# One transposed reciprocal row and one result tile per attention unit

## The chip, the cores and the metric

The kernel runs on one core of a Trainium2 chip. The metric is device time in microseconds (us) of one execution. The engines that matter are TensorE (PE; PEld is its weight load), VectorE (DVE), ScalarE (ACT), GpSimd (POOL) and SyncE (SP), which issues every DMA of this kernel, in program order.

## The reference

Three stages follow one another. The attention has 4 batches, 8 heads, 576 positions and head size 64; two gated layers of 2304 tokens by 512 come after it.

```python
scores = scale * np.matmul(q, k.transpose(0, 1, 3, 2)) + bias     # bias per head, from the distance of positions
scores = scores - np.max(scores, axis=-1, keepdims=True)
attn = np.exp(scores)
attn = attn / (np.sum(attn, axis=-1, keepdims=True) + 1e-09)
x = np.matmul(attn, v)                                            # to (2304, 512)
h = x @ w_in;  x = (h - np.tanh(h)) @ w_out                       # 512 -> 2048 -> 512
y = (1 / (1 + np.exp(-(x @ w_gate))) * (x @ w_val)) @ w_out2      # 512 -> 1536 -> 512
```

All is float32. Where products are split into a high and a low part, that is the kernel's way to keep the precision.

## The kernel before, in words

The attention works on 16 units; a unit is a pair of heads (`hp`, 0 to 3) of one batch (`b`, 0 to 3). The 2 x 576 query rows of a unit are cut into 9 tiles of 128 rows: tiles 0 to 7 are four blocks of 128 rows of the two heads in turn, tile 8 holds the last 64 rows of both. A unit takes five steps (`STEP_TILES`): two tiles in each of the first four, tile 8 in the fifth. The loop over `sg` counts steps; one pass issues work of several units in a fixed lag, so that while one unit's scores are multiplied (`scores`, L226), the step before gets its exponentials (`expo`, L247), the one three steps back is transposed (`transposes`, L278 and L284), the one four steps back is copied from PSUM (`settle`, L297, `settle5`, L302), and the product with v is run in small portions (`pv_steps`, L314 and L317). There is no scheduler: each engine runs its instructions in the order of this code and waits where data or a buffer is not ready.

`expo` also sums the exponentials of each row. `stats` (L252, L253) takes 1/(sum + 1e-9) three times a unit, for tiles 0 to 3, tiles 4 to 7 and tile 8. The value of a row then stands on the row's partition, while the product with v has the rows along its columns. So `stats` stores the values, 4 bytes each, to a scratch array `rec` in DRAM (L258 twice for each group of four tiles, L256 twice for tile 8), and `spread` loads them back as rows, one for each head, each to 64 partitions (L263, tile `rt`): 256 columns for tiles 0 to 3, 320 for the rest. `evac` copies the product from PSUM (L321), multiplies it by `rt` on POOL (L322) and stores it to `xs` (L324), for the 256 and the 320 columns apart.

The raw q and k of a unit are loaded (L171) two units ahead, into one buffer each: ACT casts them to the high part (`high`, L183) in the first and second step of the unit before, POOL subtracts for the low part (`low`, L187) two steps later, and the load of the next raw array follows that subtraction. v is loaded at L177. In the units with `b` = 3, number 3, 7 and 11, the bias tiles of the next pair of heads are loaded from DRAM too (L164, 13 DMAs). Each unit also loads and splits one block of weights for the later layers (L487). `PVN`, `KIND`, `PREP` and the lags in the loop set which piece goes into which step.

The layers that follow (L567 on) load `xs`, and run on PE nearly without a gap.

Of the kernel before, what the change touches and what calls it, by code (L numbers as in the profile page):

```python
# [7 lines left out]
F32 = mybir.dt.float32  # L8
# [3 lines left out]
AF = mybir.ActivationFunctionType  # L12
# [119 lines left out]
NU = NP * NB  # L132
STEP_TILES = ((0, 1), (2, 3), (4, 5), (6, 7), (8,))
NS = len(STEP_TILES)
PREP = {0: ("high", 0), 1: ("high", 1), 2: ("low", 0), 3: ("low", 1)}
GROUP = (0, 0, 1, 1, 2)
GW = (256, 320)
QK = S + 64

# [1 line left out]
def attention_phase(tc, qT, kT, vP, ident_d, par, c_log, bsc, recs, xs, after_bias, load_weight, filler, tail):  # L141
# [4 lines left out]
    V, A, G, T = nc.vector, nc.scalar, nc.gpsimd, nc.tensor  # L146
    with ExitStack() as st, ExitStack() as early:
        right = lambda n, k: st.enter_context(tc.tile_pool(name=n, bufs=k, side="right"))
        vp, np_, sm, xp, rp = right("p1v", 3), right("p1n", NBUF - 1), right("p1m", 4), right("p1x", 2), right("p1r", 2)
        left = lambda n, k: early.enter_context(tc.tile_pool(name=n, bufs=k))  # L150
        after_bias()
        bp, qp, stg = left("p1b", 1), left("p1q", 2), left("p1s", 1)
# [58 lines left out]
        for _ in range(ALONE):  # L211
            next(bias_steps)

        npair, n8, ntile, nmin, nsum, rt, sc, at, tr, tf = ({} for _ in range(10))

        def scores(u, s):
            (qh, ql), (kh, kl) = prep[u]
# [10 lines left out]
        def reduce_min(u, t):  # L228
            s = sc.pop((u, t))
            if t == 8:  # L230
                n = n8[u] = np_.tile([128, S], F32, name="n8", bufs=1)
            else:
                if t % 2 == 0:
                    npair[u, t // 2] = np_.tile([128, 2 * S], F32, name="n")
                n = npair[u, t // 2][:, S * (t % 2):S * (t % 2) + S]
            if t % 4 == 0:
                nmin[u, t // 4] = sm.tile([128, 4], F32, name="mn")
                nsum[u, t // 4] = sm.tile([128, 4], F32, name="sums")
            m = nmin[u, t // 4][:, t % 4:t % 4 + 1]
            V.tensor_tensor_reduce(n.rearrange("p (a b) -> p a b", a=2), s[:, :, 0:288],  # L240
                                   bias[t].rearrange("p (a b) -> p a b", a=2), -0.125, 3.0e38, ALU.add, ALU.min, m)
            ntile[u, t] = n

        def expo(u, t):
            n = ntile.pop((u, t))
            m = nmin[u, t // 4][:, t % 4:t % 4 + 1]
            A.activation(n, n, AF.Exp, bias=m, scale=-1.0, accum_out=nsum[u, t // 4][:, t % 4:t % 4 + 1])  # L247

        def stats(u, g):
            w = 1 if g == 2 else 4  # L250
            r = sm.tile([128, 4], F32, name="rec")
            V.tensor_scalar(r[:, 0:w], nsum[u, g][:, 0:w], 1e-9, None, ALU.add)  # L252
            V.reciprocal(r[:, 0:w], r[:, 0:w])  # L253
            for a in range(2):
                if g == 2:
                    nc.sync.dma_start(dram_ap(recs[u, 1], GW[1] * a + 256, [[1, 64], [1, 1]]), r[64 * a:64 * a + 64, 0:1])  # L256
                else:
                    nc.sync.dma_start(dram_ap(recs[u, g], GW[g] * a, [[1, 128], [128, 2]]), r[:, a:4:2])  # L258

        def spread(u, g):  # L260

            r = rt[u, g] = rp.tile([128, 320], F32, name="rt")
            nc.sync.dma_start(r[:, 0:GW[g]], dram_ap(recs[u, g], 0, [[GW[g], 2], [0, D], [1, GW[g]]]))  # L263

        def transposes(u, s):


            t = STEP_TILES[s][0]
            if t in (0, 4):
                w = 2 * GW[t // 4]  # L270
                at[u, t // 4] = [at_pool.tile([128, 4, w], F32, name=f"at{t}"), at_pool.tile([128, w // 2], F32, name=f"a5{t}")]
            half = (slice(0, 64), slice(64, 128))
            pt = [ps_t.tile([128, 4, 2, 64], F32, name="pt") for _ in range(2)]
            n = n8.pop(u) if s == 4 else npair.pop((u, s))
            for i in range(4):
                for x in (0,) if s == 4 else (0, S + 64):
                    for r in range(2):
                        T.transpose(pt[r][:, i, x // S], n[half[r], x + 128 * i:x + 128 * i + 128], ident[half[r], half[r]])  # L278
            if s == 4:
                for a in range(2):  # L280
                    T.matmul(tf[u, 8][half[a], 128:192], n[:, 512:S], ident[:, half[a]], start=True, stop=True)
            else:
                pf = tf[u, min(t + 1, 7) + (t + 1) // 7] = ps_f.tile([128, 192], F32, name="pf")
                T.transpose(pf[:, 0:128], n[:, 512:640], ident)  # L284
            tr[u, s] = pt

        def place5(w, t):
# [16 lines left out]
        def pv_steps(u, g):  # L304
            hp, b = units[u]
            v = vs.pop(u) if g else vs[u]
            main, rest = at[u, g]
            N = GW[g]
            p = []

            def mm(c):
                if c == 0:
                    p.append(ps_v.tile([128, 512], F32, name="pv"))
                    T.matmul(p[0][:, 0:N], v[:, 4].rearrange("p a d -> p (a d)"), rest, start=True, stop=False)  # L314
                    return
                for a in range(2):
                    T.matmul(p[0][64 * a:64 * a + 64, 0:N], v[:, c - 1, a], main[:, c - 1, a * N:a * N + N], start=False, stop=(c == 4))  # L317

            def evac():
                x = xp.tile([128, 320], F32, name="x")  # L320
                A.copy(x[:, 0:N], p[0][:, 0:N])  # L321
                G.tensor_tensor(x[:, 0:N], x[:, 0:N], rt.pop((u, g))[:, 0:N], ALU.mult)  # L322
                c0 = b * S + 256 * g
                nc.sync.dma_start(xs[128 * hp:128 * hp + 128, c0:c0 + N], x[:, 0:N])  # L324
            return [lambda c=c: mm(c) for c in range(5)] + [evac]

        pvq, late = [], []
        for sg in range(NU * NS + TAIL):
            u, s = divmod(sg, NS)
            if sg == 3:  # L330
                assert next(bias_steps, 1) == 1
                p0.close()
                at_pool = right("p1a", 1)
                ps_t, ps_f, ps_v = psr(st, "ps_t", 2), psr(st, "ps_f", 1), psr(st, "ps_v", 1)

            def at_lag(lag):
                z = sg - lag
                return divmod(z, NS) if 0 <= z < NU * NS else None
            for f in late:
                f()  # L340
            late = []
            z = at_lag(4)
            if z:
                for t in STEP_TILES[z[1]]:
                    settle5(z[0], t)
                settle(*z)
            if sg < NU * NS:
                filler(s, "V")
            y = at_lag(2)
            if y and y[1] in (1, 3, 4):  # L350
                stats(y[0], GROUP[y[1]])
            x = at_lag(3)
            if x and x[1] in (1, 4):
                spread(x[0], x[1] // 4)
            y = at_lag(1)
            if y:
                for t in STEP_TILES[y[1]]:
                    expo(y[0], t)
            if sg < NU * NS:
                scores(u, s)  # L360
                for _ in range(PER[sg] if sg < NS else 0):
                    next(bias_steps, None)
                hp, b = units[u]
                for t in STEP_TILES[s]:
                    reduce_min(u, t)
                    if b == NB - 1 and hp + 1 < NP:
                        load_bias(hp + 1, t)
            y = at_lag(3)
            if z and z[1] in (1, 4):
                pvq += pv_steps(z[0], z[1] // 4)  # L370
            steps = PVN[s] if sg < NU * NS + 3 else 5
            if y:
                transposes(*y)
            for _ in range(steps):
                if pvq:
                    pvq.pop(0)()
                    if pvq and pvq[0].__name__ == "evac":
                        late.append(pvq.pop(0))
                        break
            if s == 0 and u + 1 < NU:  # L380
                alloc(u + 1)
            if s == 3 and u + 1 < NU:
                load_v(u + 1)
            if s in PREP and 1 <= u + 1 < NU:
                k, i = PREP[s]
                if k == "high":
                    high(u + 1, i)
                else:
                    low(u + 1, i)
                    if u + 2 < NU:  # L390
                        load_raw(u + 2, i)
            if sg < NU * NS:
                filler(s, "AGv")
            if sg == NU * NS:
                early.close()
            tail(sg - NU * NS)
# [392 lines left out]
def tile_attention_then_two_mlps(ctx: ExitStack, tc: tile.TileContext, qT, kT, vP, par, wi, wo, wg, wv, wo2, c_log, ident, out, xs=None):  # L789
# [3 lines left out]
    if xs is None:  # L793
        xs = dp.tile([DM, NT], F32, name="xs")
    x2s = dp.tile([DM, NT], F32, name="x2s")
    recs = {(u, g): dp.tile([2, GW[g]], F32, name=f"rec{u}_{g}") for u in range(NU) for g in range(2)}
    with tc.manual_schedule():
        con = ctx.enter_context(tc.tile_pool(name="con", bufs=1))
        cst = []
# [100 lines left out]
```

## Time and profile before

| what | value |
|---|---|
| median of 3 runs (lowest, highest) | 1359.73 us (1355.46, 1360.43) |
| the profiled execution's own time | 1357.28 us |
| its span in the trace | 1355.1 us |
| PE busy | 1176.0 us, 87% |
| DVE, ACT, POOL busy | 682.6, 619.2, 428.3 us |
| DMA | 117.22 MB, 97394 packets, of them 28560 under 512 B |

Times in the trace are microseconds from the start of the span. A busy share is an average over stages with different limits, so the stretch from 72 to 502 us, in which the units of the attention run, is to be read apart from the rest. A wait is put down to the one that came last; "issue" in a chain or a wait means that nothing in the profile explains it. In the page's slices PE is full only in the second half:

```
PE   5676386577757589999999999999999999999998
PEclk9887688777877799999999999999999999999999
DMA  6677867766886632333334333243110101000000
```

Each digit is a fortieth of the span in tenths: the share in which PE was busy, the granted TensorE clock, and the share in which the DMA engines were busy.

### The profile page before, as it was taken

The numbers are of one execution on the slowest core, as the hardware profiler recorded it, in microseconds if no ns is written. First come the engines' busy times: TensorE is split into PE (matmuls) and PEld (weight loads), VectorE is DVE, ScalarE is ACT, GpSimd is POOL, SyncE is SP. The second block draws the span as 40 slices with busy tenths as digits, with TensorE's granted clock in tenths as the row PEclk, the third lists the DMA queues.
The fourth block names the chain that finished last, engine by engine and source line by source line (L and its number), as shares of the span: only waits on it lengthen the run. The fifth ranks groups of instructions, "written<-read, shape, count | busy, mean of one in ns | idle before, by whom it ended". The sixth has DMA issues, their size and how long they took to land.

```text
span 1355.1 us, 20411 instructions
## 1 busy us (share of the span) xinstructions
PE 1176.0 (87%) x7760; PEld 1023.8 (76%) x7760; DVE 682.6 (50%) x1222; ACT 619.2 (46%) x1241; POOL 428.3 (32%) x391
## 2 busy tenths in 40 slices
PE   5676386577757589999999999999999999999998
PEld 2254254344434369999999999999999999999997
DVE  8954255335534439888888886687410000000000
ACT  7955264354435447777776665643221121211111
POOL 1012122122212225555555553445412121212211
PEclk9887688777877799999999999999999999999999
DMA  6677867766886632333334333243110101000000
GB/s 223 235 109 83 127 87 102 109 114 89 97 120 89 72 64 70 111 111 114 116 111 142 125 127 110 73 132 113 45 41 7 36 13 35 12 19 29 1 24 24
DMA packets 97394, 117.22 MB, mean 86 GB/s; under 512 B 28560, under 2 KB 75920, under 8 KB 97296
## 3 DMA queue, kind: packets, MB, share of 16 engines
q1 hardware_dynamic: 97296, 115.92, 39.1%
q8 instruction: 61, 1.00, 0.3%
q14 instruction: 37, 0.30, 0.1%
HBM read 86.04 MB, written 29.84 MB: 86 GB/s over the span
## 4 chain that ended last, share of the span: by engine, by line
PE 64%; DMA 3%; DVE 1%; ACT 1%; issue 0%; SPq 0%; POOL 0%; DVEq 0%; ACTq 0%
PE up L584 36%; PE acc L663 14%; PE acc L671 11%; DMA xm<-xs 1%; PE pv L317 1%; DMA rec<-rec 1%; DMA raw<-in_qT 1%; PE sc L226 1%; PE pt L278 0%; ACT z L605 0%; DMA wraw<-in_wv 0%; DVE up L630 0%; DVE t L627 0%; DVE up L625 0%; DVE up L628 0%
## 5 line engine op out<-in xcount | busy, mean ns | idle before, releaser
L584 PE MATMUL up<-xt,w 128*128 128x384 f32 x2880 | 520.6, 335 | 0.6 <-DVE t L631 0.6
L584 PEld LDWEIGHTS up<-xt,w 128*128 128x128 f32 x2880 | 503.3, 188 | 8.5 <-issue 1.8
L641 POOL TENSOR_TENSOR gl<-t,gh 128x384 fp32r<-128x384 f32 x168 | 175.6, 1055 | 471.6 <-ACT gh L640 337.5
L663 PE MATMUL acc<-gh,w 128*128 128x384 f32 x768 | 195.7, 335 | 2.9 <-ACT z L605 2.9
L633 DVE TENSOR_TENSOR t<-up,t 128x384 f32<-128x384 f32 x72 | 40.0, 556 | 309.4 <-ACT t L612 309.4
L612 ACT ACTIVATE t<-up 128x384 f32<-128x384 f32 x72 | 35.4, 492 | 339.7 <-PE up L584 339.7
L278 PE MATMUL pt<-ident,n 64*128 64x64 f32 x1152 | 63.0, 248 | 123.3 <-ACT at L297 123.1
L240 DVE CUSTOM_DVE_ANT_0 n<-sc,bias 128x576 f32<-128x576 f32 x144 | 104.0, 754 | 127.0 <-PE sc L226 105.9
L278 PEld LDWEIGHTS pt<-ident,n 64*128 64x128 f32 x1152 | 54.0, 156 | 133.9 <-ACT at L297 127.9
L663 PEld LDWEIGHTS acc<-gh,w 128*128 128x128 f32 x768 | 138.1, 188 | 4.8 <-ACT z L605 3.8
L671 PE MATMUL acc<-w,gh 128*128 128x512 f32 x432 | 134.3, 392 | 0.0
L663 PE MATMUL acc<-gl,w 128*128 128x384 f32 x384 | 128.3, 334 | 0.0
L322 POOL TENSOR_TENSOR x<-x,rt 128x256 f32<-128x256 f32 (+1 forms) x32 | 25.6, 799 | 291.2 <-ACT x L321 216.4
L247 ACT ACTIVATE n<-n,mn 128x576 f32<-128x576 f32 x144 | 111.7, 784 | 3.9 <-DVE mn L240 3.9
L527 POOL TENSOR_TENSOR w<-wu,w 128x512 fp32r<-128x512 f32 x68 | 96.5, 1421 | 6.4 <-ACT w L529 6.4
L317 PE MATMUL pv<-at,vs 128*64 128x320 f32 (+1 forms) x512 | 95.3, 491 | 0.2 <-DVE at L294 0.2
L574 POOL TENSOR_TENSOR xt<-xm,xt 128x384 fp32r<-128x384 f32 x72 | 73.8, 1039 | 66.7 <-ACT xt L573 66.7
L671 PEld LDWEIGHTS acc<-w,gh 128*128 128x128 f32 x432 | 80.1, 188 | 13.5
L640 ACT CAST gh<-t 128x384 fp32r<-128x384 f32 x168 | 84.8, 511 | 8.5 <-PE acc L663 3.6
L297 DVE COPY at<-pt 128x512 f32<-128x512 f32 x64 | 44.0, 687 | 86.7 <-PE pt L278 81.3
L671 PE MATMUL acc<-w,gl 128*128 128x512 f32 x216 | 85.4, 395 | 0.0
L626 ACT ACTIVATE z<-z,c 128x768 f32<-128x768 f32 x48 | 45.2, 941 | 77.4 <-DVE up L625 77.4
(69 smaller groups left out, 1560.6 us busy)
## 6 DMA issues: line engine op xcount, KB each, us to landing
wraw<-in_wo SPq DMA_DIRECT2D x28, 512.0 KB
bsc<-e SPq DMA_DIRECT2D x36, 295.5 KB
xm<-xs SPq DMA_DIRECT2D x48, 192.0 KB
x2s<-o SPq DMA_DIRECT2D x48, 192.0 KB
wraw<-in_wi SPq DMA_DIRECT2D x16, 512.0 KB
wraw<-in_wg SPq DMA_DIRECT2D x12, 512.0 KB
wraw<-in_wv SPq DMA_DIRECT2D x12, 512.0 KB
raw<-in_qT SPq DMA_DIRECT2D x16, 320.0 KB
```

Of the source, the lines that this page charges most:

```text
L240: V.tensor_tensor_reduce(n.rearrange("p (a b) -> p a b", a=2), s[:, :, 0:288], bias[t].rearrange("p (a b) -> p a b", a=2), -0.125, 3.0e38, ...
L247: A.activation(n, n, AF.Exp, bias=m, scale=-1.0, accum_out=nsum[u, t // 4][:, t % 4:t % 4 + 1])
L278: T.transpose(pt[r][:, i, x // S], n[half[r], x + 128 * i:x + 128 * i + 128], ident[half[r], half[r]])
L317: T.matmul(p[0][64 * a:64 * a + 64, 0:N], v[:, c - 1, a], main[:, c - 1, a * N:a * N + N], start=False, stop=(c == 4))
L527: self.nc.gpsimd.tensor_sub(w[:, 1], u, w[:, 0].bitcast(F32))
L574: G.tensor_sub(t[:, 1], m, t[:, 0].bitcast(F32))
L584: T.matmul(p[:, 0:TB], w[:, a, 128 * kt:128 * kt + 128], x[:, c], start=(kt == 0 and i == 0), stop=(kt == 3 and i == 2))
L626: A.activation(z, z, AF.Relu, bias=nz, scale=-1.0)
L640: A.copy(h, x[:, j])
L641: G.tensor_sub(l, x[:, j], h.bitcast(F32))
L663: T.matmul(ac[blk][d][:, 0:TB], w[:, a, 128 * d:128 * d + 128], c, start=(begin and j == 0 and i == 0), stop=(end and j == NPR - 1 and i = ...
L671: T.matmul(ac[blk][d], g[:, c], w[:, a], start=(begin and i == 0), stop=(end and i == 2))
```

## The change

1/sum is now taken once a unit for all nine tiles, as 9 columns of one tile (`stats`); `COL` gives the column of each tile, so that a head's four tiles stand side by side. One TensorE transpose turns the 128 x 9 values into 9 rows of 128 in the PSUM tile that the unit's last full transpose uses anyway. `flat` copies these rows to SBUF on ACT and stores them in three DMAs: four rows of 512 bytes for each head, and the last row in two pieces of 256 bytes. `spread` loads them back in one DMA of 576 columns. The product with v is copied into one tile of 576 columns from two PSUM tiles; `close` multiplies it once and stores it once. `flat`, `spread` and `close` come 7, 8 and 11 steps after a unit's first, so in the third and fourth step of the next unit and the second of the one after it. The pools of the two tiles are opened later, once the bias phase has closed.

```diff
-            if t % 4 == 0:
-                nmin[u, t // 4] = sm.tile([128, 4], F32, name="mn")
-                nsum[u, t // 4] = sm.tile([128, 4], F32, name="sums")
+            if t == 0:
+                nmin[u], nsum[u] = (sm.tile([128, 9], F32, name=x) for x in ("mn", "sums"))
...
-        def stats(u, g):
-            w = 1 if g == 2 else 4
-            r = sm.tile([128, 4], F32, name="rec")
-            V.tensor_scalar(r[:, 0:w], nsum[u, g][:, 0:w], 1e-9, None, ALU.add)
-            V.reciprocal(r[:, 0:w], r[:, 0:w])
+        def stats(u):
+            r = nrec[u] = sm.tile([128, 9], F32, name="rec", bufs=2)
+            V.tensor_scalar(r, nsum.pop(u), 1e-9, None, ALU.add)
+            V.reciprocal(r, r)
+        def flat(u):
+            r = xp.tile([9, 128], F32, name="rr")
+            A.copy(r, tf[u, 8][0:9, 192:320])
             for a in range(2):
-                if g == 2:
-                    nc.sync.dma_start(dram_ap(recs[u, 1], GW[1] * a + 256, [[1, 64], [1, 1]]), r[64 * a:64 * a + 64, 0:1])
-                else:
-                    nc.sync.dma_start(dram_ap(recs[u, g], GW[g] * a, [[1, 128], [128, 2]]), r[:, a:4:2])
-        def spread(u, g):
-            r = rt[u, g] = rp.tile([128, 320], F32, name="rt")
-            nc.sync.dma_start(r[:, 0:GW[g]], dram_ap(recs[u, g], 0, [[GW[g], 2], [0, D], [1, GW[g]]]))
+                nc.sync.dma_start(dram_ap(recs[u], S * a, [[128, 4], [1, 128]]), r[4 * a:4 * a + 4])
+            nc.sync.dma_start(dram_ap(recs[u], 512, [[0, 1], [S, 2], [1, 64]]), r[8:9].rearrange("p (a q) -> p a q", a=2))
+        def spread(u):
+            r = rt[u] = rp.tile([128, S], F32, name="rt")
+            nc.sync.dma_start(r, dram_ap(recs[u], 0, [[S, 2], [0, D], [1, S]]))
+        def close(u):
+            hp, b = units[u]
+            x = xo.pop(u)
+            G.tensor_tensor(x, x, rt.pop(u), ALU.mult)
+            nc.sync.dma_start(xs[128 * hp:128 * hp + 128, b * S:b * S + S], x)
...
                 T.transpose(pf[:, 0:128], n[:, 512:640], ident)
+                if s == 3:
+                    T.transpose(pf[0:9, 192:320], nrec.pop(u), ident)
...
             def evac():
-                x = xp.tile([128, 320], F32, name="x")
-                A.copy(x[:, 0:N], p[0][:, 0:N])
-                G.tensor_tensor(x[:, 0:N], x[:, 0:N], rt.pop((u, g))[:, 0:N], ALU.mult)
-                c0 = b * S + 256 * g
-                nc.sync.dma_start(xs[128 * hp:128 * hp + 128, c0:c0 + N], x[:, 0:N])
+                if g == 0:
+                    xo[u] = xp.tile([128, S], F32, name="x")
+                A.copy(xo[u][:, 256 * g:256 * g + N], p[0][:, 0:N])
...
-            if y and y[1] in (1, 3, 4):
-                stats(y[0], GROUP[y[1]])
-            x = at_lag(3)
-            if x and x[1] in (1, 4):
-                spread(x[0], x[1] // 4)
+            if y and y[1] == 4:
+                stats(y[0])
+            for lag, f in ((7, flat), (8, spread), (11, close)):
+                x = sg - lag
+                if 0 <= x < NU * NS and x % NS == 0:
+                    f(x // NS)
```

The queue of SyncE around unit 8's reciprocals, before: `rec_0_80` and `rec_1_81` are the two scratch arrays of unit 8, `raw`, `vs` the loads of q, k and v for later units, `wraw` a weight block.

```order
L258 DMA rec_0_80<-rec 128x2x1 x2
L177 DMA vs<-in_vP 128x640
L171 DMA raw_3227<-in_kT 128x640
L263 DMA rt<-rec_0_80 128x1x256
L258 DMA rec_1_81<-rec 128x2x1 x2
L324 DMA xs<-x 128x320
L256 DMA rec_1_81<-rec 64x1 x2
L487 DMA wraw<-in_wo 128x1024
L263 DMA rt<-rec_1_81 128x1x320
L171 DMA raw_3439<-in_qT 128x640
L324 DMA xs<-x 128x256
```

The same place of the same queue in the changed kernel (`rec_72` is unit 8's scratch array, `rr` the nine rows; its lines have moved by a few numbers, L494 is L487 of before, L269 is L324).

```order
L269 DMA xs<-x 128x576
L494 DMA wraw<-in_wo 128x1024
L257 DMA rec_72<-rr 4x128 x2
L258 DMA rec_72<-rr 2x1x64
L171 DMA raw_3287<-in_qT 128x640
L263 DMA rt<-rec_72 128x1x576
L177 DMA vs<-in_vP 128x640
L171 DMA raw_3344<-in_kT 128x640
L269 DMA xs<-x 128x576
```

Six stores of `rec`, two loads of `rt` and two stores of `xs` have become three, one and one. The load of raw q, which stood behind a load of `rt`, now stands ahead of it; v and raw k stand right behind it. The first store of `rec` has moved from ahead of v to behind the weight block.

On ACT, around the cast of kh in a unit, before (`at` is the copy of transposed tiles, `n` and `sums` the exponentials, `x` the copy of the product):

```order
L183 CAST kh<-raw_2108 128x640
L297 COPY at_2186<-pt 128x8x64
L247 ACTIVATE n,sums<-n,mn 128x576 x2
L321 COPY x<-pv 128x256
```

The same place now:

```order
L183 CAST kh<-raw_2026 128x640
L305 COPY at_2095<-pt 128x8x64
L255 COPY rr<-pf 9x128
L245 ACTIVATE n,sums<-n,mn 128x576 x2
L330 COPY x<-pv 128x256
```

The copy of the nine rows has come in behind the cast of kh and one copy of `at`; the rest has kept its order.

## Rows read from the trace of the kernel before

**Rows 1.** Stretches: us, their length, busy us of engines (instructions), granted clock, DMA share, GB/s.

```profile
72.06:447.38 375.32, 248.67 (x2377) 166.10 (x2376) 173.58 (x465) 178.84 (x449) 89.85 (x83) 0.78 0.73 100
441.29:455.91 14.62, 14.62 (x173) 10.14 (x171) 11.82 (x35) 11.47 (x30) 5.02 (x5) 1.00 0.67 63
...
501.83:1355.10 853.27, 846.01 (x4644) 815.38 (x4644) 426.28 (x561) 358.60 (x627) 320.11 (x289) 1.00 0.21 70
```

**Rows 2.** Waits, 72.06 to 447.38: engine, line, for what, total us, times, longest.

```profile
ACT qh L183 <- DMA raw<-in_qT: 117.5, 13, 23.3
ACT kh L183 <- DMA raw<-in_kT: 45.1, 13, 8.5
...
PE pt L278 <- ACT at L297: 120.3, 23, 19.5
...
SPq L263 <- DMA rec<-rec: 179.6, 31, 8.8
```

**Rows 3.** Timeline of an ordinary unit: start, us, instruction, [idle before, releaser].

```profile
194.40 1.14 SPq L256 DMA_DIRECT2D rec<-rec  x2
...
204.55 0.55 SPq L263 DMA_DIRECT2D rt<-rec  x1
...
211.59 0.72 ACT L183 CAST qh<-raw 128x640 fp32r<-128x640 f32 x1 [6.71 <-DMA raw<-in_qT]
```

**Rows 4.** Timeline of SyncE, DVE and ACT at the first rec stores.

```profile
71.83 1.16 SPq L164 DMA_DIRECT2D bias<-bsc  x2
73.10 0.53 SPq L171 DMA_DIRECT2D raw<-in_qT  x1
73.73 0.89 SPq L258 DMA_DIRECT2D rec<-rec  x2
...
75.17 0.43 SPq L171 DMA_DIRECT2D raw<-in_kT  x1
83.23 0.61 SPq L263 DMA_DIRECT2D rt<-rec  x1
...
76.03 0.76 DVE L240 CUSTOM_DVE_ANT_0 n<-sc,bias 128x576 f32<-128x576 f32 x1 [4.93 <-DMA bias<-bsc]
...
77.60 0.71 ACT L183 CAST qh<-raw 128x640 fp32r<-128x640 f32 x1
...
86.19 0.72 ACT L183 CAST kh<-raw 128x640 fp32r<-128x640 f32 x1 [3.97 <-DMA raw<-in_kT]
```

**Rows 5.** Stretches of one us around them; the last two columns are DMA.

```profile
68.00:69.00 1.00, 1.00 (x25) 1.00 (x24) 0.16 (x2) 1.00 (x4) 0.00 (x0) 1.00 1.04 399
...
80.00:81.00 1.00, 1.00 (x4) 0.35 (x5) 1.00 (x3) 1.00 (x3) 0.00 (x0) 0.50 0.44 10
...
86.00:87.00 1.00, 0.00 (x0) 0.00 (x0) 0.13 (x2) 0.81 (x2) 0.00 (x0) 1.00 0.27 50
```

**Rows 6.** Groups by line and form, 72.06 to 447.38: busy us, mean ns, idle before.

```profile
L297 ACT COPY at<-pt 128x512 f32<-128x512 f32 x57 | 33.9, 595 | 0.0
...
L284 PE MATMUL pf<-ident,n 128*128 128x128 f32 x57 | 20.8, 364 | 0.0
L302 ACT COPY a<-pf 128x128 f32<-128x128 f32 x43 | 11.5, 268 | 3.2 <-PE pf L284 3.2
L322 POOL TENSOR_TENSOR x<-x,rt 128x320 f32<-128x320 f32 x13 | 11.2, 861 | 136.1 <-ACT x L321 136.1
L322 POOL TENSOR_TENSOR x<-x,rt 128x256 f32<-128x256 f32 x14 | 10.3, 735 | 129.8 <-ACT x L321 61.7 <-DMA rt<-rec 30.6 <-ACT n L247 17.1
```

**Rows 7.** Timeline: a load of rt and the multiplication that waits for it.

```profile
192.28 0.52 SPq L263 DMA_DIRECT2D rt<-rec  x1
...
202.49 0.73 POOL L322 TENSOR_TENSOR x<-x,rt 128x256 f32<-128x256 f32 x1 [10.64 <-DMA rt<-rec]
```

**Rows 8.** Unit 15: a stretch as in rows 1, and ACT's timeline.

```profile
455.91:475.77 19.86, 4.29 (x37) 2.32 (x35) 2.67 (x9) 3.54 (x9) 2.67 (x3) 0.60 0.64 80
...
470.99 0.51 ACT L573 CAST xt<-xm 128x384 fp32r<-128x384 f32 x1 [16.43 <-DMA xm<-xs]
```

More of the change, by code (lines that the diff above doesn't have):

```diff
@@ L135 @@
 PREP = {0: ("high", 0), 1: ("high", 1), 2: ("low", 0), 3: ("low", 1)}
-GROUP = (0, 0, 1, 1, 2)
+COL = [slice(c, c + 1) for c in (0, 4, 1, 5, 2, 6, 3, 7, 8)]
 GW = (256, 320)
@@ L148, in attention_phase @@
         right = lambda n, k: st.enter_context(tc.tile_pool(name=n, bufs=k, side="right"))
-        vp, np_, sm, xp, rp = right("p1v", 3), right("p1n", NBUF - 1), right("p1m", 4), right("p1x", 2), right("p1r", 2)
+        vp, np_, sm = right("p1v", 3), right("p1n", NBUF - 1), right("p1m", 4)
         left = lambda n, k: early.enter_context(tc.tile_pool(name=n, bufs=k))
@@ L212, in attention_phase @@
             next(bias_steps)
-        npair, n8, ntile, nmin, nsum, rt, sc, at, tr, tf = ({} for _ in range(10))
+        npair, n8, ntile, nmin, nsum, nrec, rt, xo, sc, at, tr, tf = ({} for _ in range(12))
         def scores(u, s):
@@ L235, in reduce_min @@
                 n = npair[u, t // 2][:, S * (t % 2):S * (t % 2) + S]
-            if t % 4 == 0:
-                nmin[u, t // 4] = sm.tile([128, 4], F32, name="mn")
-                nsum[u, t // 4] = sm.tile([128, 4], F32, name="sums")
-            m = nmin[u, t // 4][:, t % 4:t % 4 + 1]
+            if t == 0:
+                nmin[u], nsum[u] = (sm.tile([128, 9], F32, name=x) for x in ("mn", "sums"))
+            m = nmin[u][:, COL[t]]
             V.tensor_tensor_reduce(n.rearrange("p (a b) -> p a b", a=2), s[:, :, 0:288],
@@ L245, in expo @@
             n = ntile.pop((u, t))
-            m = nmin[u, t // 4][:, t % 4:t % 4 + 1]
-            A.activation(n, n, AF.Exp, bias=m, scale=-1.0, accum_out=nsum[u, t // 4][:, t % 4:t % 4 + 1])
-        def stats(u, g):
-            w = 1 if g == 2 else 4
-            r = sm.tile([128, 4], F32, name="rec")
-            V.tensor_scalar(r[:, 0:w], nsum[u, g][:, 0:w], 1e-9, None, ALU.add)
-            V.reciprocal(r[:, 0:w], r[:, 0:w])
-            for a in range(2):
-                if g == 2:
-                    nc.sync.dma_start(dram_ap(recs[u, 1], GW[1] * a + 256, [[1, 64], [1, 1]]), r[64 * a:64 * a + 64, 0:1])
-                else:
-                    nc.sync.dma_start(dram_ap(recs[u, g], GW[g] * a, [[1, 128], [128, 2]]), r[:, a:4:2])
-        def spread(u, g):
-            r = rt[u, g] = rp.tile([128, 320], F32, name="rt")
-            nc.sync.dma_start(r[:, 0:GW[g]], dram_ap(recs[u, g], 0, [[GW[g], 2], [0, D], [1, GW[g]]]))
+            A.activation(n, n, AF.Exp, bias=nmin[u][:, COL[t]], scale=-1.0, accum_out=nsum[u][:, COL[t]])
+        def stats(u):
[5 more added lines that the diff above has]
+            A.copy(r, tf[u, 8][0:9, 192:320])
+            for a in range(2):
+                nc.sync.dma_start(dram_ap(recs[u], S * a, [[128, 4], [1, 128]]), r[4 * a:4 * a + 4])
[8 more added lines that the diff above has]
+            nc.sync.dma_start(xs[128 * hp:128 * hp + 128, b * S:b * S + S], x)
         def transposes(u, s):
@@ L282, in transposes @@
             else:
-                pf = tf[u, min(t + 1, 7) + (t + 1) // 7] = ps_f.tile([128, 192], F32, name="pf")
+                pf = tf[u, min(t + 1, 7) + (t + 1) // 7] = ps_f.tile([128, 320], F32, name="pf")
                 T.transpose(pf[:, 0:128], n[:, 512:640], ident)
+                if s == 3:
+                    T.transpose(pf[0:9, 192:320], nrec.pop(u), ident)
             tr[u, s] = pt
@@ L332, in attention_phase @@
                 p0.close()
-                at_pool = right("p1a", 1)
+                at_pool, xp, rp = right("p1a", 1), right("p1x", 2), right("p1r", 2)
                 ps_t, ps_f, ps_v = psr(st, "ps_t", 2), psr(st, "ps_f", 1), psr(st, "ps_v", 1)
@@ L795, in tile_attention_then_two_mlps @@
     x2s = dp.tile([DM, NT], F32, name="x2s")
-    recs = {(u, g): dp.tile([2, GW[g]], F32, name=f"rec{u}_{g}") for u in range(NU) for g in range(2)}
+    recs = [dp.tile([2, S], F32, name=f"rec{u}") for u in range(NU)]
     with tc.manual_schedule():
```

## The prediction

> **What bounds the kernel now.** I read the slices of the page first (where is TensorE not full), then stretches one by one, then each engine's waits in the stretch that is not full, then SyncE's queue there, and last the DMA traffic at a place where little else runs.
>
> From 501.83 us to the end PE is busy 846.01 of 853.27 us at granted clock 1.00 [rows 1]. The change does not touch that part. What is open lies before it: units 1 to 14 of the attention take 375.32 us, 26.8 us each, with PE busy 248.67 us at a mean clock of 0.78. One unit's worth there shows what is needed when nothing is late: from 441.29 to 455.91, five steps, PE is busy all 14.62 us at clock 1.00, ACT 11.47, DVE 11.82. So about 12 us of each unit is waiting.
>
> The waits name the cause. ACT stands 117.5 us before the cast of qh and 45.1 us before that of kh, both for raw q and k from DRAM, 13 times each; PE then stands 120.3 us for the copy of `at` that is queued behind those casts on ACT [rows 2]. SyncE, which issues all DMAs in order, stands 179.6 us at L263 (the spread load of 1/sum) for the small stores of `rec` [rows 2]. The two belong together: in an ordinary unit the last rec stores are issued by 195.54, the load of rt can go only at 204.55, raw q is loaded behind it, and qh starts at 211.59 after 6.71 us of idleness [rows 3].
>
> What a rec store costs is seen where the first ones go out, before any rt load exists [rows 4]. The bias loads issued by 72.99 have let DVE start at 76.03: landed within 3.0 us. Raw q, issued by 73.63, is there when ACT comes to it at 77.60: at most 4.0 us. Then two rec stores (1 KB each) are issued by 74.62; rt waits for them until 83.23, 8.6 us. Raw k, queued behind them and issued by 75.60, lets kh start at 86.19, 10.6 us. Traffic was 399 GB/s at 68 us and is 10 GB/s at 80, with two 320 KB loads (v and raw k) outstanding [rows 5]. So a scatter of 4-byte elements holds not itself alone but whatever is queued behind it. A unit has three such groups (two stores each), and 26.8 us is about three times 8.6.
>
> **The change, part by part.** *Removed:* six rec stores a unit with 1152 pieces of 4 B (2 x 256, 2 x 256, 2 x 64), one of two rt loads, one of two multiplications, one of two xs stores. *Added:* three stores of 10 pieces (8 of 512 B, 2 of 256 B), one PE transpose, one ACT copy. *Moved:* raw q now goes before the rt load; v and raw k go right behind it.
>
> The stalls of traffic go with the 4-byte pieces. What is late next is a round through ACT and SyncE, in the order of the two queues: kh cast 0.72 [rows 4], `at` copy 0.595 and copy of rr (as the 128-column copy of a, 0.268) [rows 6], three rec stores (0.89 for two, so 1.35) [rows 4], rec lands, rt issue 0.55 [rows 3], v and raw k 0.43 each [rows 4], raw k lands behind rt, kh cast of the next unit. The fixed part is 0.72 + 0.595 + 0.268 + 1.35 + 0.55 + 0.86 = 4.35, say 4.4 us. Raw q's issue lies beside the landing of rec.
>
> - Landing of rec: between 3.0 us (the bias load) and 8.6 us (rec now). I take 3.0: pieces of 512 B are nearer to the rows of the loads than 4 B. With the other end a unit is 5.6 us longer and the kernel, by the sum below, ends at 1280.
> - Landing of raw k. It queues behind rt, now 576 x 128 x 4 B = 295 KB. The first rt load, 128 KB, running nearly alone, moves 50 GB/s at 86 us [rows 5], far under 399; 295 KB take 5.9 us at that. With 3.0 us for the rest of a landing this is 8.9 us from rt's issue; raw k is issued 0.86 us later and its share comes after rt's, some 0.4 us: 8.5 us from its own issue. Ends: 4.0 us (as raw q in rows 4, if it does not queue behind rt), and 21.8 us: an rt load issued by 192.80 freed POOL only at 202.49, 9.7 us for 128 KB [rows 7], times 2.25. I take 8.5, because that 9.7 lies among rec stores.
>
> Two rules of one page, the Trainium skill, "DMA: Bandwidth & Descriptors", bear on these two lines. Its Specifications say that pieces under 512 B are handled by read-modify-write. The trace agrees in direction, 8.6 us for 4 B against 3.0 us [rows 4]. It speaks against the third new store, whose pieces have 256 B; the sum by it is the one with the other end, 1280. On why a DMA increments its semaphore by 16 it says that a DMA is spread over the largest number of engines up to 16 that divides the outermost sizes of both sides: for rt that is 2, whatever its width. The trace agrees with few engines, 50 of 399 GB/s [rows 5]. By it the wide load stays on two engines, and the sum is as it stands.
>
> The round is 4.4 + 3.0 + 8.5 = 15.9 us. A second one is as long: rt lands (8.9), one multiplication of 576 columns on POOL (0.735 us for 256 and 0.861 for 320 [rows 6] continue to 1.4), xs and weight issue about 0.5 each, three rec stores 1.35, landing 3.0, rt issue 0.55: 16.2 us, the same within what its terms are known to, so I keep 15.9. Here the new waits show: the multiplication waits for rt on POOL, with the subtraction of ql behind it and so the next raw q load; the xs store waits for it on SyncE, with the weight and rec stores behind.
>
> Costed at nothing: the transpose (0.364 us as the 128-column transpose of pf [rows 6]) makes PE's floor 14.62 + 0.36 = 14.98, hidden by 0.9 us of the round; were that cover gone, it would cost 14 x 0.36 = 5 us. DVE loses four of six small operations; the evacuations stay two a unit.
>
> Sum for units 1 to 14: 14 x 15.9 = 222.6. Units 3, 7 and 11 also load the next heads' bias, 13 DMAs of 2592 KB; at 399 GB/s that is 6.5 us, of which I put half beside other work: 3 x 3 = 9. Together 231.6 against 375.32: -143.7 us. In unit 15 the step from 455.91 to 475.77 takes 19.86 us in place of some 3 (five steps in 14.62), while ACT waits 16.43 us for xm [rows 8, 1]. With 3.0 us for each of the two loads in turn about 5 of the 16.9 us excess stay: -12. The profiled execution took 1357.28 us (span 1355.1), 2.45 under the median 1359.73. 1357.3 - 143.7 - 12 = 1201.6, so 1202 us.
>
> **The rivals.**
> 1. *TensorE's floor.* If raw k does not lag behind rt, units take 14.98 us and bias hides: 14 x 14.98 = 209.7, so -165.6, and -14 in the tail: 1178. For it: the unit at 441.29 [rows 1]. Against it: the 50 GB/s of rt [rows 5].
> 2. *The wide rt load sets the pace.* At half of 50 GB/s, beside other loads on its engines, rt takes 5.9 us more and a unit 21.8: 14 x 21.8 + 9 = 314, so -61, tail -8: 1288. With a third more rt time a unit is 17.9 and the kernel 1230. For it: 9.7 us for 128 KB [rows 7]. Against it: that load ran among rec stores.
> 3. *The stores' size was not the cause.* Loads land late because of the amount of data; the DMA share is 0.73 over the stretch. Bytes hardly change, so 1345 to 1360. Against it: 399 GB/s at 68 and 100 on average [rows 5, 1].
> 4. *Slower.* One transfer now gates v, raw k, xs and the next rec stores. If rt scales from 9.7 to 21.8 us and rec keeps 8.6, a unit is 4.4 + 8.6 + 21.4 = 34.4: 14 x 34.4 = 482, +106: 1463. It decides from a unit of 26.8 us on, that is, from both landings together over 22.4 us; my sum has 11.5.
>
> **How the numbers follow.** Forecast 0.50 (its own range 1187 to 1222, a unit of 15 to 17 us), floor 0.17, wide rt 0.23, no cause 0.05, slower 0.05. About 0.5%, 6.8 us, is what a measurement of this kernel can tell from no change. Faster holds the first three, 0.90, and 0.01 of rival 3, whose other 0.04 go to same; slower has 0.05. The range goes from just under rival 1 (1176) to 1280, where the other end of rec's landing and most of rival 2 are in; some 0.13 is left out.
>
> **What would show it.** Right: SyncE waits 2 to 4 us at L263, not up to 8.8; the qh wait is gone and a kh wait of 1 to 3 us a unit is left; units of 15 to 17 us with PE's granted clock near 1.00; the part with PE full as long as now, 853 us. Wrong: L263 still waits 8 us (rival 3, or the 256 B pieces); POOL's multiplication waits over 10 us for rt and kh over 5 us (rival 2); units over 26.8 us (rival 4).

## The result and the profile after

| | before | changed |
|---|---|---|
| median, us (lowest, highest) | 1359.35 (1355.46, 1360.43) | 1225.91 (1220.19, 1233.28) |
| ratio, 95% interval | | 0.9026 (0.8968 to 0.9084) |
| profiled execution, us (span) | 1357.28 (1355.1) | 1229.55 (1227.3) |

Forecast were 1202 us and a range of 1176 to 1280; the narrower 1187 to 1222, to which the prediction gave 0.50, was missed by 4 us. The spans differ by 127.8 us. The stretches, as in [rows 1] and [rows 8], say where. The first row is units 1 to 14, the second unit 15 until PE is full, the third the rest.

```profile
73.70:335.95 262.25, 228.10 (x2391) 155.19 (x2390) 176.57 (x409) 181.85 (x464) 92.51 (x69) 0.90 0.49 145
...
335.95:374.03 38.08, 32.77 (x297) 22.31 (x296) 20.84 (x40) 20.45 (x51) 9.01 (x9) 0.96 0.29 89
374.03:1227.30 853.27, 845.93 (x4644) 815.31 (x4643) 425.55 (x561) 358.91 (x627) 321.10 (x289) 1.00 0.22 70
```

Units 1 to 14 went from 375.32 to 262.25 (-113.1), unit 15 and the passage to the layers from 54.45 (447.38 to 501.83) to 38.08 (-16.4), the rest stayed at 853.27, and the first part is 1.6 longer: together -127.8. The gain is where it was looked for, but a unit takes 18.7 us in the mean and not 15.9 to 16.5.

The waits of the changed kernel in that stretch, as in [rows 2] (L250 is the reciprocal, L292 the transpose of the reciprocals, L268 the multiplication):

```profile
ACT kh L183 <- DMA raw<-in_kT: 17.5, 6, 4.5
...
PE pt L284 <- ACT at L305: 17.1, 7, 4.0
PE pf L292 <- DVE rec L250: 13.0, 6, 2.4
...
SPq L263 <- DMA rec<-rr: 19.0, 14, 2.9
...
POOL x L268 <- DMA rt<-rec: 32.4, 6, 6.9
```

The wait of qh (117.5 us) is gone, kh's is 17.5 for 45.1, SyncE's at L263 19.0 for 179.6. New is the third row: PE waits for the reciprocals.

The chain of waits gives the landings themselves at the end of unit 14, each from the start of its issue (start, us, what):

```profile
317.79 8.79 DMA raw<-in_kT
328.68 2.86 DMA rec<-rr
331.60 8.18 DMA rt<-rec
```

I had put 8.5, 3.0 and 8.9 for these three. So these terms of the round were right; the 2.86 is the third new store, with its 256-byte pieces. What was wrong is what a unit loses beside the round. Three units, from the step in which their scores begin:

```profile
169.71:185.58 15.87, 15.04 (x175) 10.23 (x173) 12.58 (x29) 12.97 (x35) 6.87 (x6) 1.00 0.41 124
243.64:263.77 20.13, 17.77 (x175) 11.85 (x173) 13.78 (x29) 12.91 (x35) 6.77 (x6) 0.83 0.35 108
282.27:303.12 20.85, 17.51 (x174) 11.79 (x173) 12.22 (x29) 13.51 (x35) 7.03 (x6) 0.84 0.57 160
```

Unit 6 takes 15.87 at clock 1.00; unit 10 takes 20.13 with the same instructions at a mean granted clock of 0.83; unit 12, the one behind a bias unit, 20.85 at 0.84. In unit 10 this happens on GpSimd, VectorE and PE (timeline, three engines; L520 is a step of the weight split):

```profile
246.99 1.41 POOL L268 TENSOR_TENSOR x<-x,rt 128x576 f32<-128x576 f32 x1 [3.12 <-DMA rt<-rec]
247.14 1.81 DVE L520 SCALAR_TENSOR_TENSOR wu<-wraw,wu 128x512 int32<-128x512 int32 x1
248.36 1.98 POOL L187 TENSOR_TENSOR ql<-raw,qh 128x640 fp32r<-128x640 f32 x1
...
248.88 1.50 DVE L249 TENSOR_SCALAR rec<-sums 128x9 f32<-128x9 f32 x1
...
250.68 0.38 PE L292 MATMUL pf<-ident,rec 128*9 128x128 f32 x1 [2.36 <-DVE rec L250]
```

An operation on 128 x 9 elements takes 1.50 us and ends at 250.38, within 0.04 us of the subtraction of ql on GpSimd. It took 1.50 us in six of units 1 to 14, and each time it began about half a microsecond into that subtraction; in the other eight it took 0.17. The Trainium skill, "SBUF — State Buffer", Who interferes with whom, says that VectorE and GpSimd share one pair of ports as an exclusive lock held for a whole instruction, and that a `tensor_scalar` can be among the operations that take it. By that rule the small one waits until the long one is done; the trace agrees, 1.50 us for 0.17. It is the second delay of the two: in the same six units the operation just ahead of it on VectorE, L520, takes 1.52 to 1.81 us, and 0.68 in the other eight. In unit 10 it starts 0.15 us into the multiplication of 576 columns on GpSimd. Its 1.1 us more and the small operation's 1.3 us make up the 2.36 us that PE waits.

In unit 8, behind a bias unit, it is the load of k (SyncE, then ACT):

```profile
200.22 0.52 SPq L263 DMA_DIRECT2D rt<-rec  x1
200.80 1.41 SPq L164 DMA_DIRECT2D bias<-bsc  x3
202.31 0.38 SPq L177 DMA_DIRECT2D vs<-in_vP  x1
202.78 0.38 SPq L171 DMA_DIRECT2D raw<-in_kT  x1
...
213.70 0.72 ACT L183 CAST kh<-raw 128x640 fp32r<-128x640 f32 x1 [4.53 <-DMA raw<-in_kT]
```

Raw k, behind rt and three bias loads, is there 10.5 us after its issue ended (203.16), when kh starts, and ACT waits 4.53 us.

### The profile page after: what moved, and what is told of

It reads as the page before. It is cut to its first block, busy times and chain, and to the rows that moved or that the text cites. A ratio compares the mean times of both kernels' runs of the same rounds, so it can differ in the third digit from the quotient of the medians.

```text
span 1227.3 us, 20280 instructions
## 1 busy us (share of the span) xinstructions
PE 1155.8 (94%) x7776; PEld 1011.5 (82%) x7776; DVE 685.8 (56%) x1158; ACT 622.9 (51%) x1257; POOL 431.9 (35%) x375
## 4 chain that ended last, share of the span: by engine, by line
PE 69%; DMA 3%; DVE 2%; ACT 1%; issue 0%; SPq 0%; POOL 0%; ACTq 0%; POOLq 0%; DVEq 0%
PE up L591 40%; PE acc L670 15%; PE acc L678 12%; PE pv L325 1%; DMA raw<-in_kT 1%; DMA rt<-rec 1%; DMA xm<-xs 1%; DMA rec<-rr 0%; ACT z L612 0%; PE pt L284 0%; PE sc L226 0%; DMA wraw<-in_wv 0%; DVE t L634 0%; DVE up L637 0%; DVE up L632 0%
## 5 line engine op out<-in xcount | busy, mean ns | idle before, releaser
L325 PE MATMUL pv<-at,vs 128*64 128x320 f32 (+1 forms) x512 | 88.5, 462 | 0.2 <-DVE at L302 0.2
L634 DVE TENSOR_TENSOR t<-up,t 128x768 f32<-128x768 f32 x48 | 45.9, 957 | 68.5 <-ACT t L612 68.5
L284 PE MATMUL pt<-ident,n 64*128 64x64 f32 x1152 | 55.8, 234 | 19.6 <-ACT at L305 19.3
L284 PEld LDWEIGHTS pt<-ident,n 64*128 64x128 f32 x1152 | 49.6, 146 | 27.2 <-ACT at L305 21.2
L670 PEld LDWEIGHTS acc<-gl,w 128*128 128x128 f32 x384 | 72.1, 188 | 0.0
```

What stands on the lines that cost most here:

```text
L634: return [lambda: V.tensor_sub(t, p, t), lambda: V.scalar_tensor_tensor(p, z, C_LEAD, p, ALU.mult, ALU.mult), flag, lambda: V.scalar_tenso ...
L670: T.matmul(ac[blk][d][:, 0:TB], w[:, a, 128 * d:128 * d + 128], c, start=(begin and j == 0 and i == 0), stop=(end and j == NPR - 1 and i = ...
```

## The experiments

Theory A: what a unit takes over 16 us comes from two waits that the change left or made, the reciprocals held up by GpSimd (L292) and raw k behind the wide rt load, and from PE's clock, which falls after some of them. Theory B: it is the amount of data in flight, which no edit of the order changes. Three further runs take the change apart, to see what brought the gain.

**The changed kernel again** (for the same chip as the next three).

> The changed kernel once more, on the chip of the next three. Both theories: 1215 to 1235 us, units 1 to 14 some 255 to 265 us.

Measured: 1227.36 us (1223.9 to 1229.76), units 1 to 14 258.66 us.

**The reciprocals first.** The two operations of `stats` move to the head of their step:

```diff
+            y = at_lag(2)
+            if y and y[1] == 4:
+                stats(y[0])
             for f in late:
...
             if sg < NU * NS:
                 filler(s, "V")
-            y = at_lag(2)
-            if y and y[1] == 4:
-                stats(y[0])
```

> The two small operations of stats moved to the start of their step, ahead of the tile copies and the weight conversion on VectorE. Theory A (in 6 of 14 units TensorE stands about 2.1 us for the reciprocals, because their first operation takes 1.5 us in place of 0.17 beside a GpSimd operation, and the clock falls after it): no wait of TensorE at the transpose of the reciprocals, that operation back at 0.17 us in most units, those units at 15.9 to 16.5 us; 1225 becomes 1208 to 1216. Theory B (what is over 16 us in a unit is late data alone): the wait goes, but the kh wait takes its place, 1220 to 1230.

Measured: 1215.04 us (1213.2 to 1218.25), ratio to before 0.893 (0.8904 to 0.8956). The operation and the wait that takes the first place (rows of the view by tile, and of the waits):

```profile
L249 DVE TENSOR_SCALAR rec<-sums x16: 165/167/172, 80.9 to 340.3; 128x9 f32<-128x9 f32 x16
...
ACT kh L183 <- DMA raw<-in_kT: 28.3, 10, 6.1
```

It is back at 0.167 us in all 16 units, and PE no longer waits at L292. Units 1 to 14 take 248.98 us; ten of them lie between 15.5 and 16.6, but units 4, 8 and 12, each behind a bias unit, at 22.1 to 22.9, and unit 1 at 20.9. Theory A in size; its rival was right in that part of the loss reappears as a kh wait.

**The rt load in two, one for each head.**

```diff
-            nc.sync.dma_start(r, dram_ap(recs[u], 0, [[S, 2], [0, D], [1, S]]))
+            for a in range(2):
+                nc.sync.dma_start(r[64 * a:64 * a + 64], dram_ap(recs[u], S * a, [[0, D], [1, S]]))
```

> The spread load of 1/sum as two loads, one for each head (64 partitions each), so that the outermost size is 64 and not 2. Theory A (the load runs on few engines, and raw k lands behind it 9 us after its issue): rt and raw k land 3 to 4 us after their issue, the kh wait goes, the wait for the reciprocals stays or shows in more units; units of 17 us, 1200 to 1212. Theory B (raw k is late because of the amount of data): as before the edit, 1220 to 1230, and kh still waits.

Measured: 1213.46 us (1210.35 to 1216.7), 0.8916 (0.8888 to 0.8944). The waits:

```profile
PE pf L293 <- DVE rec L250: 27.6, 13, 2.2
...
ACT kh L183 <- DMA raw<-in_kT: 2.7, 1, 2.7
```

The kh wait is down from 17.5 us (21.4 in the run of the changed kernel on this chip) to 2.7 us with the same bytes, so it was the shape of one load and not the amount of data. And the wait for the reciprocals is now in 13 units and not in 6: with k in time, the subtraction of ql meets them in nearly every unit. From unit 2 on, units take 17.0 us at clock 1.00 (unit 12, with the kh wait, 18.2) and 18.5 to 19.9 where the clock fell.

**Both.**

> Both edits. Theory A: units at TensorE's floor, 15.0 to 15.5 us, clock near 1.00 from unit 2 on, bias units not over 16; 1172 to 1190. Theory B: 1215 to 1230.

Measured: 1192.01 us (1191.28 to 1193.12), 0.8761 (0.8735 to 0.8787). Units 1 to 14, and a stretch of one unit's length; the third row is unit 11 in the run of the changed kernel again:

```profile
72.72:301.37 228.65, 217.72 (x2391) 147.23 (x2390) 175.82 (x409) 181.26 (x464) 93.85 (x69) 0.99 0.54 166
...
156.20:172.25 16.05, 15.53 (x175) 10.45 (x171) 12.77 (x29) 12.85 (x34) 6.80 (x5) 1.00 0.43 132
...
256.57:271.73 15.16, 15.16 (x174) 10.34 (x172) 11.87 (x29) 13.07 (x35) 7.00 (x6) 1.00 0.70 214
```

From unit 2 on every unit takes 15.6 to 16.5 us, those with bias loads too. Each edit alone brought 12 and 14 us, both 35 (1227.36 to 1192.01), because each uncovers the other's wait. The time is 2 us over what theory A gave, since units settle at 16.05 and not at 15.0 to 15.5. That is not the least a unit can take: in the third row PE is busy all 15.16 us. The four executions of this run lie within 2 us; those of the changed kernel spread over 13, and its two profiles show the waits on different units.

**GpSimd's order turned**, to test the cause of the 1.50 us with the reciprocals left where the change has them: `close` runs one step later, behind the subtraction of ql.

```diff
-            for lag, f in ((7, flat), (8, spread), (11, close)):
+            for lag, f in ((7, flat), (8, spread)):
...
+            x = sg - 12
+            if 0 <= x < NU * NS and x % NS == 0:
+                close(x // NS)
             if sg < NU * NS:
                 filler(s, "AGv")
```

> The changed kernel with one order turned: on GpSimd the subtraction of ql goes ahead of the 576-column multiplication (close comes at the end of the next step, behind it), everything else, stats too, stays in place. Theory A (the first operation of stats takes 1.5 us whenever it begins beside the subtraction of ql, and only because the multiplication has pushed that subtraction there): that operation takes 0.17 us, or less than 1 us, in most units and TensorE no longer waits for it, 1208 to 1220 us. Rival (it is slow by its place behind the weight conversion on VectorE, whatever runs on GpSimd): 1.5 us in six or more units as before, 1222 to 1232.

Measured: 1218.06 us (1215.96 to 1221.1), 0.8977 (0.8948 to 0.9007).

```profile
L249 DVE TENSOR_SCALAR rec<-sums x16: 157/161/167, 80.6 to 345.4; 128x9 f32<-128x9 f32 x16
...
PE pf L292 <- DVE rec L250: 4.2, 6, 0.8
```

At most 0.167 us in all 16 units, in the same place of VectorE's queue. So it was GpSimd's work beside it, which stood there because the one multiplication of 576 columns had come in ahead of the subtraction and waited for rt or for the evacuation. The subtraction is not the only one: in unit 10 of the changed kernel's second profile the operation takes 1.38 us beside that multiplication. Theory A holds, its rival falls. The time is little below the changed kernel's; kh now waits 30.6 us, in eight units.

**The change with 4-byte stores**: the reciprocals stored straight from their 128 x 9 tile, without the transpose and the copy (the output is the same); one load, one multiplication and one store stay.

```diff
-            A.copy(r, tf[u, 8][0:9, 192:320])
+            r = nrec.pop(u)
             for a in range(2):
-                nc.sync.dma_start(dram_ap(recs[u], S * a, [[128, 4], [1, 128]]), r[4 * a:4 * a + 4])
+                nc.sync.dma_start(dram_ap(recs[u], S * a, [[1, 128], [128, 4]]), r[:, 4 * a:4 * a + 4])
+            for a in range(2):
+                nc.sync.dma_start(dram_ap(recs[u], S * a + 512, [[1, 64], [1, 1]]), r[64 * a:64 * a + 64, 8:9])
```

> The changed kernel with the stores of 1/sum as before, in 4-byte pieces straight from the 128 x 9 tile (1152 pieces in four stores, two of 512 and two of 64), without the transpose and the ACT copy; the one load of 576 columns, the one multiplication and the one store stay. Theory A (the 4-byte pieces hold the traffic): rec lands 8 to 10 us after its issue and raw q, v, raw k behind it; units of 21 to 24 us, 1260 to 1310. Rival (the number of stores, loads and waits is what counted, not the size of the pieces): units as now, 1220 to 1235.

Measured in one run: 1315.36 us, against 1360.23 of before beside it. SyncE's timeline in one unit (L256 and L258 store rec), then SyncE's waits and the stretch of units 1 to 14:

```profile
202.76 1.12 SPq L256 DMA_DIRECT2D rec<-rec  x2
203.92 1.16 SPq L258 DMA_DIRECT2D rec<-rec  x2
205.50 0.35 SPq L171 DMA_DIRECT2D raw<-in_qT  x1
214.10 0.55 SPq L263 DMA_DIRECT2D rt<-rec  x1
```

```profile
SPq L263 <- DMA rec<-rec: 81.6, 16, 9.7
```

```profile
72.57:405.59 333.02, 246.00 (x2378) 164.26 (x2378) 161.55 (x409) 180.24 (x450) 86.88 (x69) 0.83 0.62 113
```

The stores are issued by 205.08, and rt goes at 214.10: 9.0 us, against 2.86 from the start of the last issue with rows. Units take 23.8 us, near the 24 that theory A had as its upper end; the time is 5 us above its range. The rival falls: by this one run the 4-byte pieces are worth 90 us of the 134. Whether it is their size or their number, 1152 for 10, is not told apart.

**Before, with its rt loads in two each** (the edit of the second experiment at its L263).

> The kernel before with each spread load of 1/sum as two loads, one for each head. Theory A (4-byte stores set the pace before): 1335 to 1365. Rival (the loads on few engines were half of the trouble): under 1310.

Measured in one run: 1357.38 us beside 1360.23.

```profile
SPq L264 <- DMA rec<-rec: 181.3, 33, 8.7
```

L264 is the spread load there. Its wait stands as before (179.6), and so does the time. By this one run the shape of the rt load costs nothing as long as the 4-byte stores set the pace; it came to matter only through the change.

**Before, with only the multiplication and the xs store merged** (the new `evac`, `close` and one rt tile filled by two loads; stores of 1/sum as before).

> The kernel before with only the second half of the change: the product copied into one tile of 576 columns, multiplied once and stored once, eleven steps after the unit's first; stores and loads of 1/sum as before (two loads into one tile). Theory A: the stores of 4 bytes still hold the queue, 1340 to 1370, units of 25 to 28 us. Rival (merging the multiplication and the store is what brought the time): under 1300.

Measured in one run: 1343.3 us beside 1360.23, units 1 to 14 367.92 us, 26.3 each.

```profile
SPq L264 <- DMA rec<-rec: 159.7, 29, 8.6
```

As theory A had it: merging alone leaves the wait. That it brings some 17 us of the gain stands on one run.

## Why the prediction was right, and where it was not

*The cause.* Right. The 4-byte stores held the DMA traffic, and with them SyncE's queue, ACT's casts and PE: with the pieces put back 90 of 134 us are lost again, and neither the rt loads nor the merging by themselves bring more than 17 (one run each). These parts do not add up to 134; the rest comes from parts of the change together.

*The landings.* Right within 1 us: rec 2.86 for 3.0, raw k 8.79 for 8.5, rt 8.18 for 8.9. The 50 GB/s that I took for rt beside 4-byte pieces shows again while the wide load of the three landings above runs by itself (a stretch as in [rows 1]):

```profile
337.00:338.00 1.00, 1.00 (x21) 0.70 (x17) 0.85 (x3) 0.00 (x0) 0.00 (x0) 1.00 0.13 48
```

The DMA share of 0.13 of 16 engines is that of two. What is issued behind such a load waits for it in part: of the 128 packets of v, issued next, 112 start by 334.85, and the other 16, an eighth, only from 339.17 on, when rt's own are through. With 64 in place of 2 as the load's outermost size kh's wait falls to 2.7 us. That bears out the rule on the outermost size in the Trainium skill, "DMA: Bandwidth & Descriptors", on why a DMA increments its semaphore by 16. The rule on pieces under 512 B in the Specifications of that page of the Trainium skill was no reason to fear the 256-byte pieces: the trace has 2.86 us for that store.

*The units.* The step that failed is the sum for units 1 to 14, 231.6 us against 262.25 measured. Its 15.9 for a plain unit is met in units 6 and 14 (15.87, 15.83), which is in part luck: from one cast of kh to the next it is 18.4 and 18.5 us there, with PE's wait for the reciprocals in the unit before. The round shows by itself in the run with the reciprocals first, where units 10 and 11 both wait for raw k and the casts are 15.51 us apart:

```profile
241.84 0.73 ACT L183 CAST kh<-raw 128x640 fp32r<-128x640 f32 x1 [1.37 <-DMA raw<-in_kT]
...
257.35 0.73 ACT L183 CAST kh<-raw 128x640 fp32r<-128x640 f32 x1 [1.05 <-DMA raw<-in_kT]
```

Three costs were missed or too small:

- The reciprocals, "costed at nothing" with VectorE's small operations. I counted their removal. That the subtraction of ql stands behind the moved multiplication I saw, but looked only at raw q's load; I asked neither what that does to VectorE beside it nor who waits if the reciprocals are late. PE waits at the new transpose: 13.0 us in six units.
- Bias, 3 us for each of three heads' loads (14 DMAs, not 13; the bytes are right). The unit behind a bias unit takes 20.9 to 21.1 us, 5.0 to 5.2 over a plain one, as raw k lies behind rt and the bias loads on SyncE. The bias units themselves take 18.4 to 18.5, unit 7 for raw k, units 3 and 11 for the reciprocals. With the rt load split kh waits once, 2.7 us in unit 12.
- The clock. I took units to run at 1.00. With PE's idle stretches the mean granted clock was 0.83 and 0.84 in units 10 and 12, 0.90 over all 14, and the work between runs slower. Not every such stretch did it: unit 5 has one of 2.14 us and a clock of 1.00.

Removing the first two removes nearly all of the third: 228.65 us, clock 0.99. That lies near the sum's 231.6, but by other terms: 16.0 for a plain unit, almost nothing for bias, and 20.2 us for unit 1, which I gave 15.9 though before it had the 4.93 us bias wait of [rows 4].

*The floor.* 14.98 for PE was near: two units of the changed kernel's second profile take 15.2 us, in one of them PE is busy throughout. With both edits units settle at 16.05 all the same. ACT's work is not the reason, since it is busy 13.07 us in the unit of 15.16 and 12.85 in that of 16.05. VectorE is busy 12.77 us there for 11.87; two steps of the weight split on it take 1.30 and 1.60 us in most of the units of 16.05, and 0.68 and 1.33 in that of 15.16. That this is the reason was not tried.

*Unit 15.* -12 forecast, -16.4 measured. The two loads of xm that I put at 3.0 us are 3.23 and 3.83 in the chain, so they are not where the further 4.4 us come from; what they are was not taken apart.

*The rivals.* The floor is not reached by the change itself, but for single units. The measured time lies near the 1230 of the second rival's milder case, by another mechanism. The wide rt load is half right: it does not set the pace by its bandwidth, but it delays k, most in the units with bias and behind them. Rival 3 and the slower case did not come; the landings that would have decided it, 22.4 us together, were 11.65.

## What to carry to other kernels

Look for stores of single elements first where an in-order DMA queue waits: what they cost is not their bytes but everything queued behind them, and turning them into rows took a transpose of 0.27 us of PE a unit here. When such a stall goes, write down for each small operation that was hidden who will wait for it and what GpSimd runs beside it; a few tenths of a microsecond became two here, on the engine that was now the bound, and in four of six units its clock fell. And when two waits cover each other, remove both before judging either: 12 and 14 us alone were 35 together.

## What the runs showed of the hardware that was not expected

- A VectorE operation on 128 x 9 float32 elements takes 0.17 us, and 1.50 us when it starts half a microsecond into a 128 x 640 subtraction on GpSimd; it ends with that subtraction, which itself takes 1.98 in place of 1.55 us in these units. A 128 x 512 operation with two inputs takes 1.52 to 1.81 us in place of 0.68 beside the multiplication ahead of it.
- Four stores with 1152 pieces of 4 bytes hold a wait for them 9.0 us; with three of 10 pieces of 256 and 512 bytes the last lands 2.86 us after its issue began.
- A spread load of 295 KB whose outermost size is 2 lands in 8.18 us and moves 48 GB/s by itself, at a DMA share of 0.13. As two loads of 64 partitions it lets raw k land in time with the same bytes.
